# Hash attention and two MLPs on one core: the sums of weights leave GpSimd, and ScalarE scales the low words of float64

## The chip, the cores and the metric

The kernel runs on one NeuronCore of a Trainium2 chip. The metric is the device time of one execution in microseconds; for the kernel before it is the median of three runs. TensorE is PE in the profile, its weight loads are PEld, VectorE is DVE, ScalarE is ACT, GpSimd is POOL and the engine that issues the DMAs is SP. Every engine works through its own queue in order, so an instruction that waits holds everything behind it on that engine.

## The reference

Three parts follow each other. The first, an attention with a hash mask, gives `x` of 1536 tokens by 512. The second and the third are two MLPs, and the change lies in the second part, the first MLP, which also prepares the weights of the third.

```python
def _moe_ref(x, w_gate, w_val, w_out):            # first MLP: 512 -> 1536 -> 512
    g = x @ w_gate
    silu = g * (1.0 / (1.0 + np.exp(-g)))
    val = x @ w_val
    return (silu * val @ w_out).astype(np.float32)

def _moe2_ref(x, w_in, w_out, g_ln):              # second MLP: 512 -> 1024 -> 512
    h = x @ w_in
    e = np.exp(h - np.max(h, axis=-1, keepdims=True))
    solu = h * e / (np.sum(e, axis=-1, keepdims=True) + 1e-09)
    mu = np.mean(solu, axis=-1, keepdims=True)
    var = np.mean((solu - mu) ** 2, axis=-1, keepdims=True)
    ln = (solu - mu) / np.sqrt(var + 1e-06) * g_ln
    return (ln @ w_out).astype(np.float32)
```

The weights arrive as float64. The kernel computes each matmul as three matmuls of a high and a low part (high by high, high by low, low by high).

## The kernel before

**First MLP.** The hidden width of 1536 is cut into 12 columns of 128 (`f`), two to a stage, so there are six stages `t` = 0 to 5. The tokens are cut into three blocks of 512 (`blk`). A stage has nine units of 24 matmuls each: six hidden units (units 0 to 5: two `f` by three blocks, function `hidden`) and three sum units (`summed`, blocks 0 to 2), which multiply by `w_out`. PE runs the units one behind the other. A hidden unit fills two PSUM banks, `h0` (gate) and `h1` (value). ACT takes `silu` of `h0` (L1108), DVE multiplies by `h1` (L1109, written to `sg`), ACT rounds `sg` to `ah` (L1111), DVE forms the rest `al` (L1114). The bank pairs are doubled, so unit u+2 needs what unit u left to be read. A sum unit fills four banks `y`, one after the other, and there are only four, so the next sum unit needs them emptied: ACT copies them to `yf` in stage 0 (L1135), DVE adds them to `yf` in the later stages (L1137).

**Conversions.** Beside this runs a stream of weight conversions (`conversions`), cut into pieces of 1 MB of float64 each. Pieces "1" hold one `f` of `w_gate` and `w_val`, pieces "2" two `f` of `w_out`, pieces "3" 128 rows of the second MLP's `w_in`, pieces "4" 256 rows of its `w_out`. For each piece SP issues the load into `raw` (two buffers: the load of piece n+2 is issued when piece n is done), and `to_float32` makes float32 `wf` of it in six DVE instructions (L47, L51, L53, L57, L62, L64 by their profile names; L62 scales the low words, L64 adds them). Then ACT rounds to the high part (`hi`, L1037) and DVE forms the low part (`lo`, helper `low`, L958). The "late" pieces do more:

- Pieces "3" (`blocks3`, L960 to L993) also form sums and differences of weight blocks, `t1` to `t4`, each rounded to a high and a low part. GpSimd does the sums (L977 to L992) and the rounding (`rounded`, L1001 and L1002).
- Pieces "4" are scaled by `g_ln` (L1018), rounded by ACT (L1020), their low part is formed by GpSimd (L1021), and both parts are parked in DRAM (L1023), since they live in the piece's `raw` buffer.

**Order.** It is written out by hand: the main loop (the end of the listing's first MLP) takes steps of the stream with `go(stream)`, each step being what stands between two `yield`s of the conversion. A hidden unit takes up to four steps: one, then the `al` of the unit before, then up to three more that break off at a step that says "copied" (ACT's rounding), then silu, product and `ah` of the unit. A sum unit takes three steps, in stage 0 five. `LATE` says how many late pieces each stage gets, `late` in which order. Keys in `pieces` hold a piece back until its buffers are free: the first `f` of the next stage may start at unit 3, the second at the first sum unit.

**Ahead and behind.** At the end of the attention, PE, DVE and ACT each take one slot of about 2.1 us per block: ACT's exponential `e` (L574), PE's scores `s` (L539, two buffers), the transposes `t` (L589), ACT's `eh` (L598) and DVE's `el` (L602). Behind the first MLP, GpSimd forms sums of tokens (`sums_of`, L1001 to L1076) for the second MLP.

Of the kernel before, what the change touches and what calls it, by code (L numbers as in the profile page):

```python
# [9 lines left out]
F32 = mybir.dt.float32  # L10
R32 = mybir.dt.float32r
I32 = mybir.dt.int32
U32 = mybir.dt.uint32
# [21 lines left out]
FLOOR = 2.0 ** -15  # L35


def to_float32(nc, raw, f):

    words = raw.bitcast(I32).rearrange("p (n t) -> p n t", t=2)
    low, high = words[:, :, 0], words[:, :, 1]
    bits = f.bitcast(I32)


    nc.vector.tensor_scalar(  # L47
        bits, high, 1, 1, ALU.logical_shift_left, ALU.logical_shift_right
    )
    yield  # L50
    nc.vector.tensor_scalar_max(f, f, FLOOR)  # L51
    yield
    nc.vector.tensor_scalar(  # L53
        bits, bits, 3, 0x3FFFFFF8, ALU.logical_shift_left, ALU.bitwise_and
    )
    yield
    nc.vector.scalar_tensor_tensor(  # L57
        bits, high, -0x40000000, bits, ALU.bitwise_and, ALU.bitwise_or
    )
    yield  # L60

    nc.vector.tensor_scalar_mul(high, low.bitcast(U32), 2.0 ** -29)  # L62
    yield
    nc.vector.tensor_tensor(bits, bits, high, ALU.add)  # L64


@with_exitstack
def hash_attention_then_two_mlps(
# [150 lines left out]
    with at:  # L219
# [494 lines left out]
        def go(work):  # L714

            next(work, None)
# [182 lines left out]
    with ExitStack() as m1:  # L899
# [24 lines left out]
            nc.gpsimd.tensor_sub(lo[:, n], w1f[n], hi[:, n].bitcast(F32))  # L924

        pieces = []
        LATE = (2, 1, 1, 1, 1, 2)
        late = [("3", n) for n in (0, 2, 1, 3)] + [("4", n) for n in range(0, KF2, 2)]
        for t in range(TH):
            fs = range(t * FT, (t + 1) * FT)  # L930
            pieces += [(t - 1, FT * NBLK, "1", f) for f in fs[1:]]
# [25 lines left out]
        def low(dst, src, hi):  # L957
            nc.vector.tensor_sub(dst, src, hi.bitcast(F32))  # L958

        def blocks3(n, wf, raw):  # L960

            i, d = divmod(n, KH)
            left, right, other = wf[:, :BLK], wf[:, BLK:], w1f[d]
            b11, b21, b22, t1, t2, t3, t4 = (
                [w3_of[x][:, m, d] for m in range(2)]
                for x in ("b11", "b21", "b22", "t1", "t2", "t3", "t4")
            )
            add, sub = nc.gpsimd.tensor_add, nc.gpsimd.tensor_sub  # L970
            if i == 0:
                nc.scalar.copy(b11[0], left)
                nc.scalar.copy(other, right)
                yield "copied"
                low(b11[1], left, b11[0])
                one = raw.bitcast(F32)[:, :BLK]
                sub(one, other, b11[0].bitcast(F32))  # L977
                sub(one, one, b11[1].bitcast(F32))
                rounded(*t1, one)
                return  # L980
            nc.scalar.copy(b21[0], left)
            nc.scalar.copy(b22[0], right)
            yield "copied"
            low(b21[1], left, b21[0])
            sub(b22[1], right, b22[0].bitcast(F32))
            for block, first, t in ((b22, sub, t3), (b11, add, t2), (b21, sub, t4)):
                hi, lo = (x.bitcast(F32) for x in block)
                if first is sub:
                    sub(other, hi, other)
                else:  # L990
                    add(other, other, hi)
                add(other, other, lo)  # L992
                rounded(*t, other)  # L993

        def rounded(hi, lo, src):

# [7 lines left out]
        def convert(piece, raw):  # L1004
            kind, n = piece[2:4]
            wf = wr.tile([P, 2 * DM], F32, tag="wf", name="wf", bufs=1)
            yield from to_float32(nc, raw, wf)
            if kind == "4":

                hi, lo = (  # L1010
                    raw.bitcast(R32)[:, m * 2 * DM:(m + 1) * 2 * DM].rearrange(
                        "p (m e) -> p m e", m=2
                    ) for m in range(2)
                )
                wf = wf.rearrange("p (m e) -> p m e", m=2)
                both = lo.bitcast(F32)
                for m in range(2):
                    nc.scalar.mul(both[:, m], wf[:, m], gl[:, n + m:n + m + 1])  # L1018
                yield "copied"
                nc.scalar.copy(hi, both)  # L1020
                nc.gpsimd.tensor_sub(lo, both, hi.bitcast(F32))  # L1021
                for m, x in enumerate((hi, lo)):
                    nc.sync.dma_start(parked[m][n // 4][:, n % 4:n % 4 + 2], x.bitcast(F32))  # L1023
                return
            if kind == "3":
                yield from blocks3(n, wf, raw)
                return
            if kind == "1":
                hi, lo = weights1(n)
            else:  # L1030
                hi, lo = [
                    w2.tile([P, 2, DM], R32, tag=f"{x}2", name=f"{x}2") for x in ("hi", "lo")
                ]
                for m in range(2):
                    w2_of[n + m] = [x[:, m] for x in (hi, lo)]
            hi, lo = (x.rearrange("p m e -> p (m e)") for x in (hi, lo))
            nc.scalar.copy(hi, wf)  # L1037
            yield "copied"
            low(lo, wf, hi)
# [115 lines left out]
        for t in range(TH):  # L1155
            for unit in range((FT + 1) * NBLK):
                f, blk = divmod(unit, NBLK)
                reached = (t, unit)
                if t == TH - 1 and unit == FT * NBLK:

                    yh = xpool.tile([P, KD, NT], R32, tag="h", name="yh")
                    yl = xpool.tile([P, KD, NT], R32, tag="l", name="yl")
                    run(stream)
                    for n in (0, 2):
                        parts = halves(ws)
                        for x, stored in zip(parts, parked):
                            nc.sync.dma_start(x.bitcast(F32), stored[0][:, n:n + 2])
                        for m in range(2):
                            w4_of[n + m] = [x[:, m] for x in parts]
                    nc.scalar.activation(half, half, AF.Exp)  # L1170
                work = hidden(t * FT + f, blk) if f < FT else summed(t, blk)
                go(work)
                if f < FT:

                    go(stream)
                    go(before)
                    for _ in range(3):
                        if next(stream, None) == "copied":
                            break
                    go(work)  # L1180
                    before = work
                    continue

                go(before)
                before = lows(blk - 1) if t == TH - 1 and blk else iter(())
                for d in range(KD):
                    if blk and t == TH - 1:
                        go(before)
                    else:
                        if t == 0 or d != 1:  # L1190
                            go(stream)
                        if t == 0 and d == 1:
                            go(stream)
                    go(work)
# [265 lines left out]
```

## Time and profile before

| | |
|---|---|
| median of three runs | 700.08 us (698.76 to 700.26) |
| the profiled execution | 700.51 us, span of its instructions 698.7 us |
| attention | 0 to about 249 us |
| first MLP | about 248 to 559 us |
| second MLP | about 558 to 699 us |
| busy: PE, DVE, ACT, POOL | 679.0, 586.5, 354.8, 281.2 us |

Matmuls are pipelined: a matmul of 512 columns is shown with 0.39 us, but the next one starts 0.23 us later. So a busy PE says little; what counts is how far apart the starts of units lie, and which wait ended before a start that came late.

### The profile page before, as it was taken

What the parts mean: (1) busy time and instruction counts of PE and PEld (TensorE: products, weight loads), DVE (VectorE), ACT (ScalarE), POOL (GpSimd) and SP (SyncE); (2) the same over time, 40 slices, a digit from 0 to 9 for tenths busy, and PEclk for the clock granted to TensorE, in tenths of its full rate; (3) what the DMA queues carried; (4) which work ended last, traced back from release to release, by engine and by line L of the source; (5) the groups of instructions that cost most, each with busy time, mean ns of one, the idle gap of its engine ahead of it and who ended that gap; (6) DMA issues with size and microseconds to landing.
All of it is one profiled execution on the core that took longest, in us unless ns stands there. A gap on an engine that the chain in (4) does not pass through costs nothing. (4 is left out here: it accounts for less than half of the span.)

```text
span 698.7 us, 10396 instructions
## 1 busy us (share of the span) xinstructions
PE 679.0 (97%) x3653; PEld 583.0 (83%) x3653; DVE 586.5 (84%) x1032; ACT 354.8 (51%) x726; POOL 281.2 (40%) x285
## 2 busy tenths in 40 slices
PE   8999999999999999988899998999999999999998
PEld 6999999999998888866788886888888787888877
DVE  7989999999999997878897798886888869755781
ACT  7898898989888943332212202313222633433431
POOL 6647556666524340383030191000101575775300
PEclk9999999999999999999999999999999999999999
DMA  6683753736334112042131321243141530122211
GB/s 180 169 203 103 190 132 97 179 111 163 89 91 147 34 62 99 31 139 94 60 121 61 99 83 60 74 168 119 62 168 74 180 121 20 71 91 91 91 46 46
DMA packets 39492, 73.72 MB, mean 106 GB/s; under 512 B 5352, under 2 KB 26920, under 8 KB 38672
## 3 DMA queue, kind: packets, MB, share of 16 engines
q1 hardware_dynamic: 39440, 73.06, 34.1%
q8 instruction: 29, 0.48, 0.3%
q14 instruction: 23, 0.19, 0.1%
HBM read 40.90 MB, written 7.34 MB: 69 GB/s over the span
## 5 line engine op out<-in xcount | busy, mean ns | idle before, releaser
L1101 PE MATMUL h<-xh,hi 128*128 128x512 f32 x288 | 112.5, 391 | 6.4 <-ACT sg L1108 5.8
L1101 PE MATMUL h<-xl,hi 128*128 128x512 f32 x288 | 112.1, 389 | 0.0
L1101 PE MATMUL h<-xh,lo 128*128 128x512 f32 x288 | 111.2, 389 | 0.0
L602 DVE TENSOR_TENSOR el<-t,eh 128x384 fp32r<-128x384 f32 x192 | 97.7, 550 | 9.6 <-ACT eh L598 8.2
L574 ACT ACTIVATE e<-s,nm 128x768 f32<-128x768 f32 x96 | 97.7, 1017 | 4.5 <-DVE nm L559 3.8
L598 ACT CAST eh<-t 128x384 fp32r<-128x384 f32 x192 | 83.9, 492 | 18.5 <-PE t L589 16.8
L550 DVE TENSOR_REDUCE top<-s 128x1 f32<-128x768 f32 x96 | 90.6, 943 | 0.7 <-PE s L539 0.5
L589 PE MATMUL t<-idr,e 128*128 128x128 f32 x576 | 80.1, 274 | 0.5 <-DVE el L602 0.3
L589 PEld LDWEIGHTS t<-idr,e 128*128 128x128 f32 x576 | 67.9, 140 | 9.4 <-DVE el L602 4.0
L1101 PEld LDWEIGHTS h<-xh,hi 128*128 128x128 f32 x288 | 54.0, 188 | 19.2 <-ACT sg L1108 7.1
L624 PE MATMUL av<-eh,vs 128*128 128x384 f32 x186 | 63.9, 344 | 0.0
L1101 PEld LDWEIGHTS h<-xl,hi 128*128 128x128 f32 x288 | 54.1, 188 | 11.1
L1101 PEld LDWEIGHTS h<-xh,lo 128*128 128x128 f32 x288 | 54.0, 188 | 11.1
L1111 ACT CAST ah<-sg 128x512 fp32r<-128x512 f32 x36 | 22.4, 623 | 80.2 <-DVE sg L1109 80.2
L1037 ACT CAST hi<-wf 128x1024 fp32r<-128x1024 f32 x17 | 17.8, 1049 | 88.4 <-DVE wf L64 88.4
L1125 PE MATMUL y<-ah,hi 128*128 128x512 f32 x144 | 57.2, 397 | 4.9 <-DVE yf L1137 2.7
L1021 POOL TENSOR_TENSOR raw<-raw 128x1024 fp32r<-128x1024 f32 x4 | 9.8, 2441 | 118.4 <-ACT raw L1020 71.8
L1127 PE MATMUL y<-ah,lo 128*128 128x512 f32 x144 | 56.7, 394 | 0.0
L1126 PE MATMUL y<-al,hi 128*128 128x512 f32 x144 | 56.6, 393 | 0.0
L539 PE MATMUL s<-ka,qa 128*128 128x384 f32 x192 | 54.6, 365 | 1.6 <-ACT e L574 1.4
L628 PE MATMUL av<-el,vs 128*64 128x384 f32 x155 | 52.2, 337 | 0.0
L1109 DVE TENSOR_TENSOR sg<-h,sg 128x512 f32<-128x512 f32 x36 | 24.8, 688 | 30.7 <-ACT sg L1108 20.0
(277 smaller groups left out, 1585.6 us busy)
## 6 DMA issues: line engine op xcount, KB each, us to landing
raw<-in_moe_w_out_dram SPq DMA_DIRECT2D x10, 1024.0 KB
raw<-in_moe_w_gate_dram SPq DMA_DIRECT2D x12, 512.0 KB
raw<-in_moe_w_val_dram SPq DMA_DIRECT2D x12, 512.0 KB
ka<-kt SPq DMA_DIRECT2D x30, 192.0 KB
moved<-u SPq DMA_DIRECT2D x9, 512.0 KB
raw<-in_moe_w_in_dram SPq DMA_DIRECT2D x4, 1024.0 KB
parked<-raw SPq DMA_DIRECT2D x8, 512.0 KB
v<-in_v_dram SPq DMA_DIRECT2D x8, 384.0 KB
```

The costliest lines, as they stand in the source:

```text
L539: nc.tensor.matmul(s[:, n, :HALF], a[:, rows], m[:, n * HALF:(n + 1) * HALF], start=first, stop=not first,)
L550: nc.vector.tensor_reduce(top[:, 1:2], s_of[i][:, :, :HALF], AX.XY, ALU.max, negate=True)
L574: nc.scalar.activation(e, s_of.pop(i)[:, :, :HALF], AF.Exp, bias=nm[:, 1:2], scale=nm[:, 0:1], accum_out=total_of[p, n][:, j, c:c + 1],)
L589: nc.tensor.transpose(t[:, m, :], e_of[i][:, g, m * P:(m + 1) * P], idf)
L598: nc.scalar.copy(half_tile(eh_of, i, g), t_of[i, g])
L602: last_of[i] = nc.vector.tensor_sub(half_tile(el_of, i, g), t_of.pop((i, g)), half_tile(eh_of, i, g).bitcast(F32),)
L624: nc.tensor.matmul(av, vj[:, c], eh_of[h][:, c, :], start=c == 0, stop=c == C - 1)
L628: nc.tensor.matmul(*low, start=False, stop=False)
L1101: nc.tensor.matmul(ps[n], a[:, n, kk, :], x[:, kk, blk * BLK:(blk + 1) * BLK], start=kk == 0 and a is hi and x is xh, stop=kk == KD - 1 an ...
L1125: nc.tensor.matmul(p, hi[:, cols], ah, start=f == t * FT, stop=False)
L1126: nc.tensor.matmul(p, hi[:, cols], al, start=False, stop=False)
L1127: nc.tensor.matmul(p, lo[:, cols], ah, start=False, stop=f == (t + 1) * FT - 1)
```

## The change

- `to_float32` gets a switch. With it (all pieces of the first MLP), ACT scales the low words of `raw` in place as the first instruction of a piece, and DVE's L62 is gone. Without it (two small pieces in the attention) DVE still does it, now in place.
- `blocks3` forms all sums and differences on DVE, into `wf` and `w1f`, and ACT rounds them; GpSimd's instructions are gone. There are more `yield`s, so the work is cut into more steps.
- Pieces "4": ACT scales and rounds in one instruction for each half, DVE forms the low part with one instruction for each half.
- Late pieces come in another order: 30, 40 | 32 | 42, 44 | 31 | 33 | 46 by stage, where it was 30, 32 | 31 | 33 | 40 | 42 | 44, 46.
- A hidden unit now always takes four steps: those that a "copied" cut off come behind the unit's own work.

```diff
-def to_float32(nc, raw, f):
+def to_float32(nc, raw, f, scalar=False):
...
+    if scalar:
+        nc.scalar.mul(low, low.bitcast(U32), 2.0 ** -29)
     nc.vector.tensor_scalar(
         bits, high, 1, 1, ALU.logical_shift_left, ALU.logical_shift_right
     )
...
-    nc.vector.tensor_scalar_mul(high, low.bitcast(U32), 2.0 ** -29)
-    yield
-    nc.vector.tensor_tensor(bits, bits, high, ALU.add)
+    if not scalar:
+        nc.vector.tensor_scalar_mul(low, low.bitcast(U32), 2.0 ** -29)
+        yield
+    nc.vector.tensor_tensor(bits, bits, low, ALU.add)
...
-        LATE = (2, 1, 1, 1, 1, 2)
-        late = [("3", n) for n in (0, 2, 1, 3)] + [("4", n) for n in range(0, KF2, 2)]
+        LATE = (2, 1, 2, 1, 1, 1)
+        late = [(x[0], int(x[1])) for x in "30 40 32 42 44 31 33 46".split()]
...
-            add, sub = nc.gpsimd.tensor_add, nc.gpsimd.tensor_sub
+            add, sub = nc.vector.tensor_add, nc.vector.tensor_sub
             if i == 0:
                 nc.scalar.copy(b11[0], left)
                 nc.scalar.copy(other, right)
                 yield "copied"
                 low(b11[1], left, b11[0])
-                one = raw.bitcast(F32)[:, :BLK]
-                sub(one, other, b11[0].bitcast(F32))
-                sub(one, one, b11[1].bitcast(F32))
-                rounded(*t1, one)
+                yield
+                sub(left, right, left)
+                nc.scalar.copy(t1[0], left)
+                yield "copied"
+                low(t1[1], left, t1[0])
                 return
...
             low(b21[1], left, b21[0])
-            sub(b22[1], right, b22[0].bitcast(F32))
-            for block, first, t in ((b22, sub, t3), (b11, add, t2), (b21, sub, t4)):
...
+            yield
+            low(b22[1], right, b22[0])
+            yield
+            sub(right, right, other)
+            nc.scalar.copy(t3[0], right)
+            yield
+            add(other, right, b11[0].bitcast(F32))
+            yield
+            add(other, other, b11[1].bitcast(F32))
+            nc.scalar.copy(t2[0], other)
+            yield
+            low(t3[1], right, t3[0])
+            yield
+            sub(left, left, other)
+            nc.scalar.copy(t4[0], left)
+            yield
+            low(t2[1], other, t2[0])
+            yield "copied"
+            low(t4[1], left, t4[0])
...
-            yield from to_float32(nc, raw, wf)
+            yield from to_float32(nc, raw, wf, True)
...
-                    nc.scalar.mul(both[:, m], wf[:, m], gl[:, n + m:n + m + 1])
+                    nc.scalar.mul(hi[:, m], wf[:, m], gl[:, n + m:n + m + 1])
                 yield "copied"
-                nc.scalar.copy(hi, both)
-                nc.gpsimd.tensor_sub(lo, both, hi.bitcast(F32))
+                for m in range(2):
+                    if m:
+                        yield
+                    nc.vector.scalar_tensor_tensor(
+                        lo[:, m], wf[:, m], gl[:, n + m:n + m + 1], hi[:, m].bitcast(F32),
+                        ALU.mult, ALU.subtract,
+                    )
...
-                    for _ in range(3):
-                        if next(stream, None) == "copied":
-                            break
+                    steps = [go(stream)]
+                    while len(steps) < 3 and steps[-1] != "copied":
+                        steps.append(go(stream))
                     go(work)
+                    for _ in range(3 - len(steps)):
+                        go(stream)
```

PE's instructions stand in the same order as before. Three places show what moves on the others. Lines of the changed kernel are 2 or 3 higher than before up to `blocks3`, and 14 to 20 higher behind it.

The first place is ACT near the end of the attention, ten exponentials before the last. Before, its queue there reads:

```order
L691 COPY xf<-av 128x384
L598 CAST eh<-t 128x3x128 x2
L574 ACTIVATE e,total<-s,nm 128x768
L598 CAST eh<-t 128x3x128 x2
L574 ACTIVATE e,total<-s,nm 128x768
```

and now:

```order
L694 COPY xf<-av 128x384
L601 CAST eh<-t 128x3x128 x2
L48 ACTIVATE raw<-raw 128x1024
L577 ACTIVATE e,total<-s,nm 128x768
L601 CAST eh<-t 128x3x128 x2
```

The first piece's scaling (L48) has come between `eh` and an exponential; the DVE half of that piece still starts only when the attention's last `el` is done.

The second place is ACT in the sum units of stage 0, where ACT itself empties the banks `y`. Before, from unit 5's silu on (piece 30 gives `w3b` and `w1f`, piece 32 the next two `w3b`):

```order
L1108 ACTIVATE sg<-h_4200 128x512
L1111 CAST ah<-sg 128x512
L1135 COPY yf<-y 128x512
L972 CAST w3b_3963<-wf 128x512
L973 COPY w1f_96<-wf 128x512
L1135 COPY yf<-y 128x512 x6
L981 CAST w3b_3964<-wf 128x512
L982 CAST w3b_3965<-wf 128x512
L1135 COPY yf<-y 128x512 x5
```

and now (`w3t` is a sum of weights, `raw<-wf,gl` the scaling of piece 40, `hi` the rounding of a piece "1"):

```order
L1126 ACTIVATE sg<-h_4207 128x512
L1129 CAST ah<-sg 128x512
L981 CAST w3t_3966<-wf 128x512
L1153 COPY yf<-y 128x512
L48 ACTIVATE raw<-raw 128x1024
L1153 COPY yf<-y 128x512 x4
L1031 ACTIVATE raw<-wf,gl 128x512 x2
L1153 COPY yf<-y 128x512 x2
L48 ACTIVATE raw<-raw 128x1024
L1153 COPY yf<-y 128x512 x3
L1055 CAST hi_4370<-wf 128x1024
L1153 COPY yf<-y 128x512 x2
```

The first copy now stands behind the rounding of a sum, and scalings and roundings of three more pieces lie between the other copies.

The third place is GpSimd, whose queue before had this between the attention's last `xl` and the sums of tokens, a second time for the other half, and four `raw<-raw` behind it (the start is shown); all of it is gone:

```order
L977 TENSOR_TENSOR raw<-w1f,w3b 128x512
L978 TENSOR_TENSOR raw<-raw,w3b 128x512
L1001 TENSOR_TENSOR w3t<-raw,unit 128x512
L1002 TENSOR_TENSOR w3t<-raw,w3t 128x512
L985 TENSOR_TENSOR w3b<-wf,w3b 128x512
L989 TENSOR_TENSOR w1f<-w3b,w1f 128x512
L992 TENSOR_TENSOR w1f<-w1f,w3b 128x512
```

On DVE the sums of pieces 32 and 33 now lie between the additions to `yf` of a stage's sum units, which in stage 1 reads:

```order
L961 TENSOR_TENSOR w3b_3965<-wf,w3b_3965 128x512
L1155 TENSOR_TENSOR yf<-y,yf 128x512 x2
L992 TENSOR_TENSOR wf<-wf,w1f_96 128x512
L1155 TENSOR_TENSOR yf<-y,yf 128x512
L995 TENSOR_TENSOR w1f_96<-wf,w3b_3963 128x512
L1155 TENSOR_TENSOR yf<-y,yf 128x512
L997 TENSOR_TENSOR w1f_96<-w1f_96,w3b_3963 128x512
```

Each step between two additions is one instruction of 128x512 there, where steps of 128x1024 stood.

## Rows read from the trace of the kernel before

**Rows 1.** The page: busy us, share of the span and instructions, by engine.

```profile
PE 679.0 (97%) x3653; PEld 583.0 (83%) x3653; DVE 586.5 (84%) x1032; ACT 354.8 (51%) x726; POOL 281.2 (40%) x285
```

**Rows 2.** Timeline of PE, unit starts: start us, us shown, engine, line, operation, names.

```profile
255.00 0.39 PE L1101 MATMUL h<-xh,hi 128*128 128x512 f32 x1
...
369.62 0.39 PE L1101 MATMUL h<-xh,hi 128*128 128x512 f32 x1
...
375.06 0.39 PE L1101 MATMUL h<-xh,hi 128*128 128x512 f32 x1
...
553.12 0.39 PE L1125 MATMUL y<-ah,hi 128*128 128x512 f32 x1
```

**Rows 3.** Waits of PE, 248 to 560 us: us in total, times, longest.

```profile
PE h L1101 <- ACT sg L1108: 5.8, 3, 2.6
PE y L1125 <- DVE yf L1137: 2.7, 2, 1.9
PE y L1125 <- ACT yf L1135: 2.2, 2, 2.0
PE h L1101 <- DVE sg L1109: 0.6, 1, 0.6
```

**Rows 4.** Windows: length, busy us (instructions) PE, PEld, DVE, ACT, POOL; clock; DMA.

```profile
301.00:359.00 58.00, 52.35 (x221) 41.82 (x220) 51.65 (x56) 11.82 (x19) 25.35 (x16) 0.97 0.21 70
359.00:408.00 49.00, 49.00 (x218) 40.58 (x217) 39.58 (x51) 11.22 (x17) 8.04 (x6) 1.00 0.29 101
```

**Rows 5.** The same view, one stretch behind a wait of PE.

```profile
345.00:350.00 5.00, 3.88 (x12) 3.08 (x13) 4.92 (x8) 0.97 (x2) 0.00 (x0) 0.74 0.00 0
```

**Rows 6.** Timeline of POOL in stage 1.

```profile
305.14 1.62 POOL L1002 TENSOR_TENSOR w3t<-w1f,w3t 128x512 fp32r<-128x512 f32 x1
```

**Rows 7.** Timeline of DVE beside it.

```profile
305.65 2.20 DVE L57 SCALAR_TENSOR_TENSOR wf<-raw,wf 128x1024 int32<-128x1024 int32 x1
```

**Rows 8.** Timeline of DVE, such instructions in stage 0, POOL idle.

```profile
260.20 0.69 DVE L51 TENSOR_SCALAR wf<-wf 128x1024 f32<-128x1024 f32 x1
260.81 0.68 DVE L1109 TENSOR_TENSOR sg<-h,sg 128x512 f32<-128x512 f32 x1
...
262.80 1.22 DVE L57 SCALAR_TENSOR_TENSOR wf<-raw,wf 128x1024 int32<-128x1024 int32 x1
264.05 0.69 DVE L62 TENSOR_SCALAR raw<-raw 128x1024 int32<-128x1024 uint32 x1
264.78 1.23 DVE L64 CUSTOM_DVE_ANT_0 wf<-raw,wf 128x2048 uint16<-128x2048 uint16 x1
...
267.62 0.69 DVE L1109 TENSOR_TENSOR sg<-h,sg 128x512 f32<-128x512 f32 x1 [1.61 <-ACT sg L1108]
```

**Rows 9.** Timeline of ACT, sum units of stage 0; in brackets idle time and its end.

```profile
298.16 0.62 ACT L981 CAST w3b<-wf 128x512 fp32r<-128x512 f32 x1 [5.13 <-DVE wf L64]
```

**Rows 10.** Groups of ACT by form, 255 to 558 us: busy, mean ns, idle before.

```profile
L1037 ACT CAST hi<-wf 128x1024 fp32r<-128x1024 f32 x17 | 17.8, 1049 | 88.4 <-DVE wf L64 88.4
L1018 ACT ACTIVATE raw<-wf,gl 128x512 f32<-128x512 f32 x8 | 5.4, 716 | 16.9 <-DVE wf L64 16.9
```

**Rows 11.** Groups of DVE by form, 255 to 558 us.

```profile
L958 DVE TENSOR_TENSOR w3b<-wf,w3b 128x512 fp32r<-128x512 f32 x4 | 2.8, 693 | 1.5 <-ACT w3b L972 0.7 <-ACT w3b L981 0.7
```

**Rows 12.** Timeline of ACT where the first scaling will stand.

```profile
222.82 0.87 ACT L598 CAST eh<-t 128x384 fp32r<-128x384 f32 x2
223.56 1.03 ACT L574 ACTIVATE e<-s,nm 128x768 f32<-128x768 f32 x1
```

**Rows 13.** Timeline of PE there, the scores that reuse that exponential's buffer.

```profile
225.06 0.59 PE L539 MATMUL s<-ka,qa 128*128 128x384 f32 x2
```

**Rows 14.** Timeline of SP: the load of the first piece is issued.

```profile
219.04 0.54 SPq L944 DMA_DIRECT2D raw<-in_moe_w_gate_dram  x1
```

**Rows 15.** Windows of 1 us there; the last figure is GB/s moved.

```profile
223.00:224.00 1.00, 1.00 (x9) 0.93 (x8) 0.97 (x4) 1.00 (x3) 0.00 (x0) 1.00 1.04 319
```

**Rows 16.** Waits of PE in the second MLP.

```profile
PE o L1330 <- DVE ll L1316: 0.7, 2, 0.5
```

More of the change, by code (lines that the diff above doesn't have):

```diff
@@ L958, in low, with blocks3 @@
             nc.vector.tensor_sub(dst, src, hi.bitcast(F32))
-        def blocks3(n, wf, raw):
+        def blocks3(n, wf):
             i, d = divmod(n, KH)
@@ L984, in blocks3 @@
             low(b21[1], left, b21[0])
-            sub(b22[1], right, b22[0].bitcast(F32))
-            for block, first, t in ((b22, sub, t3), (b11, add, t2), (b21, sub, t4)):
[L987 to L993, printed above, removed]
+            yield
[17 more added lines that the diff above has]
+            low(t4[1], left, t4[0])
         def rounded(hi, lo, src):
@@ L1015, in convert @@
                 wf = wf.rearrange("p (m e) -> p m e", m=2)
-                both = lo.bitcast(F32)
                 for m in range(2):
-                    nc.scalar.mul(both[:, m], wf[:, m], gl[:, n + m:n + m + 1])
+                    nc.scalar.mul(hi[:, m], wf[:, m], gl[:, n + m:n + m + 1])
                 yield "copied"
-                nc.scalar.copy(hi, both)
-                nc.gpsimd.tensor_sub(lo, both, hi.bitcast(F32))
+                for m in range(2):
[5 more added lines that the diff above has]
+                    )
                 for m, x in enumerate((hi, lo)):
@@ L1025, in convert @@
             if kind == "3":
-                yield from blocks3(n, wf, raw)
+                yield from blocks3(n, wf)
                 return
```

## The prediction

> **What bounds the kernel now.** I began with the page [rows 1]. PE is busy for 97% of the span, but that counts the pipelined tail of each matmul, so I went on to unit starts [rows 2]. An undisturbed hidden unit takes 375.06 - 369.62 = 5.44 us for its 24 matmuls. From the second unit of the first MLP (255.00) to its last sum unit (553.12) lie 52 units. At 5.44 us they would take 282.9 us; they took 298.1. So the first MLP loses 15.2 us, and nothing that leaves PE's 24 matmuls as they are can give back more there.
>
> The list of waits [rows 3] says who is late: 5.8 + 2.7 + 2.2 + 0.6 = 11.3 us of PE's waits end with ACT's silu or copy or with DVE's product or addition. The other 3.9 us follow the waits: a matmul behind one takes longer to get going, and behind the wait at 346 us the granted clock falls to 0.74 for a stretch [rows 5], that is, part of it at 1.2 GHz.
>
> Why they are late shows in the windows. In stage 1, with POOL busy for 25 us, DVE is busy for 51.7 of 58 us and PE waits; in stage 2, with POOL busy for 8 us, DVE is busy for 39.6 of 49 and PE doesn't wait [rows 4]. A single instruction shows it: L57 takes 1.22 us alone [rows 8] and 2.20 us beside POOL [rows 7]. It began at 305.65, POOL's L1002 ended at 306.76 [rows 6], and 2.20 - 1.22 = 1.0 us of it lies before that. The two alternate, and DVE runs at about half speed for as long as POOL has sums to form. ACT stands in order behind it: its rounding waited 5.13 us for DVE [rows 9], with the copies that PE needed queued behind.
>
> **The change, part by part.**
>
> GpSimd's sums go. All of POOL's work of the first MLP's weights (34 instructions of 128x512 and four of 128x1024, counted in its queue) disappears, and with it the doubling of DVE's instructions.
>
> DVE's own load. Each of 24 pieces loses one L62 of 0.69 us [rows 8], 16.6 us in all. Added are sums and low parts of 128x512: 2 for a piece 30 or 31, 8 for 32 or 33, 2 for each of four pieces "4", so 2x2 + 2x8 + 4x2 = 28 at 0.69 [rows 11], 19.3 us. The two balance. An ordinary piece now costs DVE about 5.9 us: L47, L51, L53 at 0.73 from start to start, L57, L64 and `lo` at 1.25 [rows 8]. Stage 1 has three of these, piece 32 (4.7 + 9 x 0.69 = 10.9 us), and at 0.69 each six products with their rests and twelve additions (16.6): 45.2 us of the 48.96 that nine units last. Stage 2, with two pieces "4" (6.1 each) in place of it, has 46.5. Both fit.
>
> ACT's load. Each piece gains a scaling of 128x1024. No row has ScalarE on integer words with a stride. From below, the rounding of 128x1024 takes 1.05 us; from above I take twice the two scalings of 128x512 at 0.72 each with a second pass, 2.3 us [rows 10]. I take 1.15, since the scaling of 512 costs 0.1 more than its share of the rounding. ACT is busy for 11.8 of 58 us in stage 1 [rows 4], so as load it costs nothing; what counts is what stands behind it. The Trainium skill ("ScalarE: Activation LUTs", section "Rules for kernel authors") speaks against this move: multiplications belong on VectorE. By the same page's section "What ACT_TABLE_LOAD costs" an instruction with immediate operands would take an estimated 186 + 0.833 x 1024 = 1040 ns, so the sum below would be 0.1 us lower; that it is longer than DVE's 0.69 agrees with the rows, and it matters only where ACT is the one awaited.
>
> That is the **attention's end**, the first new cost. The scaling of the first piece comes to ACT at 223.56, when the exponential started [rows 12]. Its load was issued at 219.04 [rows 14]; by the bytes moved in windows of 1 us, of which the last that counts is [rows 15], its 1 MB is there at about 223.9. So the scaling runs from 223.95 to 225.1, the exponential ends at 226.1, and the scores that need its buffer start then and not at 225.06 [rows 13]: 1.05 us. `eh` behind it gives 0.15 more. PE has no gaps in that part, so this is lost: **+1.2 us** (0.9 with a scaling of 1.05 and no more, 2.6 with 2.3 us and the load 0.3 later).
>
> **Stage 0's sum units** keep part of their stall. The first copy of a bank now stands on ACT behind the rounding of piece 30's difference. From the end of that piece's L64 the chain is, at 0.62 for an ACT instruction of 128x512 [rows 9] and 0.6 to 0.7 for one of DVE (0.61 where the next doesn't depend on it, 260.20 to 260.81 in [rows 8]): two roundings, silu, product, low part, rest, difference, rounding, copy, some 5.6 us; the next sum unit wants the bank 5.3 us after unit 5 ends. So the stall is how late that L64 ends, plus 0.3. DVE starts this stage late: at its beginning ACT now rounds piece "1" and loads its table ahead of the first silu. A unit asks DVE for four of a piece's six steps (3.9 us) and 1.2 of product and rest, 5.1 of 5.44, and where a rounding stands ahead of a silu it idles another 1.6 [rows 8]. I walked the three queues by hand in their new order with these durations: L64 ends 1.4 us after unit 5. That gives 1.7 us, and 0.2 for a second bank: **1.9 us left** (0.3 with no delay, 4.4 with 4).
>
> **Stages 1 to 4.** The same chain ends in an addition on DVE without the extra rounding; the pieces held back to unit 3 let DVE catch up first. The walk gives the first bank 0.3 us before it is wanted, 0.1 in stage 2. I leave **0.6 us** for the four (0 to 3). The other copies and silus have 3 to 4 us to spare. The load of the piece behind a "4" waits until both halves are parked; the walk has it land 3 us before a silu behind its scaling is due.
>
> **Second MLP.** GpSimd's sums of tokens start as soon as the last low parts of block 0 are there, now about 0.8 us earlier against PE. PE's 0.7 us behind `ll` [rows 16] may shrink: **-0.4** (0 to -0.7).
>
> **Sum.** Against the profiled execution of 700.51 us: -15.2 + 1.9 + 0.6 + 1.2 - 0.4 = -11.9, so 688.6. The median lies 0.43 lower, 700.08: **688.2 us**.
>
> **The rivals.**
>
> *Scaling on ScalarE is dear* (2.3 us). For it: strided integer words, which no row has; against it: DVE reads the same words at its usual 0.69 [rows 8]. The attention loses 1.15 more, and in stage 0 the second copy comes 1.2 later than its bank is wanted. 688.2 + 2.3 = 690.5, up to 694 with other copies late.
>
> *The queues, not the doubling, make PE wait.* For it: 8 of the 11.3 us end with ACT [rows 3], and three more conversions now lie between the copies of stage 0. Against it: stage 2 has the same queues and no wait [rows 4]. Half of the 15.2 us stays, 7.6 where the forecast leaves 2.5: 688.2 + 5.1 = 693.3.
>
> *Slower: ACT turns into the bound.* Every scaling stands ahead of a silu. In the 1.5 units of a piece, 8.16 us, ACT has one rounding (1.05, [rows 10]) and 1.5 times silu and `ah` (at 0.62 each 1.9), so 5.2 us are free. Should an integer scaling take more, PE waits for the excess 24 times: at 7 us, 24 x 1.8 = 43, about 731. It decides the sign from 5.7 us on (24 x 0.5 = 12). Against it: a rounding of the same size takes 1.05 us. A load that lands later than 8 us after its issue would act the same way.
>
> *It doesn't do what it says:* what the sums give, waits on loads behind parked pieces take back; about 700.
>
> **How the numbers follow.** Forecast 0.62, dear scaling 0.15, queues 0.10, slower 0.08, no change 0.05. What a measurement can tell apart is 0.2%, 1.4 us. The first three are faster: 0.87; same 0.05; slower 0.08. The forecast's own bounds: against 700.08, -15.2 + 0.3 + 0.9 - 0.7 = -14.7, so 685.4; and -15.2 + 4.4 + 3 + 2.6 = -5.2, so 694.9. That takes in the first two rivals but for their tails. The range is 685 to 695.5.
>
> **What would show it.** Right: DVE's L57 and its like at 1.22 us through stages 1 and 3; PE's waits in the first MLP about 2 us, nearly all in stage 0 at a `y` bank; clock 1.00 throughout; scores about 1 us late once at 225 us; the scaling at 1.1 to 1.2 us. Wrong: a scaling over 2 us; PE waiting in stages 1 to 4 for a silu behind a scaling; or DVE's instructions still stretched with POOL idle.

## The result and the profile after

The changed kernel takes 689.54 us (median of four, 687.92 to 690.89), the kernel before 699.42 in the same comparison: ratio 0.986 [0.983, 0.989]. Timed again it was 688.68 against 701.36, 0.982 [0.980, 0.984]. Its profiled execution took 687.92 us, 12.6 less than the 700.51 of before. Below, the page of the changed kernel: its busy line (to compare with [rows 1]), POOL's slices of the span, and the chain that ended last. A line of the changed kernel has a number 2 to 20 higher than the same line before.

```profile
PE 675.5 (98%) x3653; PEld 582.4 (85%) x3653; DVE 563.5 (82%) x1035; ACT 381.8 (56%) x755; POOL 216.7 (32%) x247
...
POOL 6647555666624260000000000000000574775200
...
PE 85%; DVE 8%; ACT 3%; issue 2%; DMA 1%; POOL 0%; SPq 0%; ACTq 0%; DVEq 0%; POOLq 0%
```

POOL is idle through the first MLP, and the chain is PE's own work for 85%. The waits of PE in the first MLP are down from four groups with 11.3 us [rows 3] to one:

```profile
PE y L1143 <- ACT yf L1153: 1.8, 1, 1.8
```

The windows of stages 1 and 2 (length; busy PE, PEld, DVE, ACT, POOL; clock; DMA) have PE busy throughout at clock 1.00, where stage 1 had 58 us [rows 4]:

```profile
299.00:348.00 49.00, 49.00 (x218) 40.58 (x217) 38.21 (x51) 19.56 (x29) 0.00 (x0) 1.00 0.34 117
348.00:397.00 49.00, 49.00 (x218) 40.58 (x217) 41.86 (x55) 16.67 (x23) 0.00 (x0) 1.00 0.31 108
```

**One number for each kernel.** As in the prediction, the loss of the first MLP is the time from the start of its second unit to that of its last sum unit, less 52 x 5.44 = 282.9 us. Before it was 15.2. Now the two starts are 255.83 and 540.97, and the loss is 2.26. The table gives it by stage for every run below. Time and ratio come from all runs of a kernel, the loss from its one traced execution. By time alone neither the kernel with fills nor the one with the sums back on GpSimd can be told from the changed kernel, since their intervals overlap; the loss tells them apart. From "changed, again" on, each four ran on one chip with their own runs of the kernel before (medians 701.36, 700.38 and 700.44 us); the ratios are against these.

| kernel | time, us | ratio [95%] | loss by stage 0 to 5 | sum |
|---|---|---|---|---|
| before | 699.42 | 1 | 2.8, 8.5, 0, 2.9, 0, 1.1 | 15.2 |
| changed | 689.54 | 0.986 [0.983, 0.989] | 2.3, 0, 0, 0, 0, 0 | 2.3 |
| changed, again | 688.68 | 0.982 [0.980, 0.984] | 2.3, 0, 0, 0, 0, 0 | 2.3 |
| first scaling on DVE | 690.92 | 0.985 [0.983, 0.986] | 5.0, 0, 0, 0, 0, 0 | 5.0 |
| rounding later | 685.90 | 0.979 [0.977, 0.980] | 0.1, 0, 0, 0, 0, 0 | 0.1 |
| both of these | 686.58 | 0.979 [0.977, 0.981] | 1.4, 0, 0, 0, 0, 0 | 1.4 |
| idle GpSimd additions | 705.44 | 1.007 [1.003, 1.011] | 7.4, 2.2, 1.5, 6.4, 2.1, 0.5 | 20.1 |
| idle GpSimd fills | 690.24 | 0.985 [0.981, 0.989] | 4.5, 0, 0, 0, 0, 0 | 4.5 |
| sums back on GpSimd | 690.41 | 0.985 [0.981, 0.989] | 4.3, 0, 0.2, 0, 0, 0 | 4.5 |
| before + scaling on ACT | 697.54 | 0.995 [0.994, 0.997] | 6.6, 1.4, 3.1, 0, 0, 0 | 11.0 |
| before + new order | 697.28 | 0.995 [0.993, 0.997] | 5.5, 2.1, 0.2, 1.6, 1.8, 0.3 | 11.4 |
| changed, old list | 693.53 | 0.990 [0.988, 0.992] | 2.3, 5.0, 0, 0, 0, 0 | 7.3 |
| changed, no scaling on ACT | 692.90 | 0.989 [0.988, 0.991] | 1.1, 0, 0, 3.9, 0, 3.4 | 8.4 |
| five scalings | 745.76 | 1.064 [1.062, 1.066] | 18.5, 7.6, 9.9, 9.3, 7.7, 4.1 | 57.1 |

### The profile page after: what moved, and what is told of

It reads as the page before. It is cut to its first block, busy times and chain, and to the rows that moved or that the text cites. A ratio compares the mean times of both kernels' runs of the same rounds, so it can differ in the third digit from the quotient of the medians.

```text
span 686.1 us, 10380 instructions
## 1 busy us (share of the span) xinstructions
PE 675.5 (98%) x3653; PEld 582.4 (85%) x3653; DVE 563.5 (82%) x1035; ACT 381.8 (56%) x755; POOL 216.7 (32%) x247
## 4 chain that ended last, share of the span: by engine, by line
PE 85%; DVE 8%; ACT 3%; issue 2%; DMA 1%; POOL 0%; SPq 0%; ACTq 0%; DVEq 0%; POOLq 0%
PE h L1119 24%; PE s L542 9%; PE t L592 8%; PE h L1235 7%; PE y L1143 5%; PE y L1144 4%; PE y L1145 4%; PE av L627 4%; PE av L631 3%; PE o L1350 3%; PE o L1348 3%; PE o L1349 3%; PE pp L501 2%; PE pp L458 2%; PE t L1329 1%
## 5 line engine op out<-in xcount | busy, mean ns | idle before, releaser
L605 DVE TENSOR_TENSOR el<-t,eh 128x384 fp32r<-128x384 f32 x192 | 97.8, 551 | 10.7 <-ACT eh L601 9.4
L1082 POOL TENSOR_TENSOR sf<-yh 128x256 f32<-128x256 f32 x5 | 3.7, 736 | 282.2 <-ACT yh L1158 282.2
L542 PE MATMUL s<-kb,qb 76*128 76x384 f32 x192 | 49.8, 339 | 0.0
```

Of the source, the lines that this page charges most:

```text
L542: nc.tensor.matmul(s[:, n, :HALF], a[:, rows], m[:, n * HALF:(n + 1) * HALF], start=first, stop=not first,)
L605: last_of[i] = nc.vector.tensor_sub(half_tile(el_of, i, g), t_of.pop((i, g)), half_tile(eh_of, i, g).bitcast(F32),)
```

## Experiments on what is left: the attention's end and stage 0

> The changed kernel as it is, timed again beside the three below, so that differences of a microsecond can be read on one chip. By its first times 687.9 to 690.9 us, ratio 0.983 to 0.989. PE's waits in the first MLP: once 1.75 us at 290.39 in front of a sum unit of stage 0, nothing in stages 1 to 5. Any other picture would say that the first trace was no typical one.

The picture is the same: one wait of 1.8 us, loss 2.25.

**The rounding in stage 0.** The timeline of ACT in the changed kernel shows the chain that the one wait ends with (start, us, engine, line, operation, names; in brackets idle time and what ended it), and behind it the matmul that waited:

```profile
284.86 0.62 ACT L975 CAST w3b<-wf 128x512 fp32r<-128x512 f32 x1 [3.15 <-DVE wf L67]
285.39 0.61 ACT L976 COPY w1f<-wf 128x512 f32<-128x512 f32 x1
285.91 0.59 ACT L1126 ACTIVATE sg<-h 128x512 f32<-128x512 f32 x1
287.26 0.62 ACT L1129 CAST ah<-sg 128x512 fp32r<-128x512 f32 x1 [0.76 <-DVE sg L1127]
289.24 0.62 ACT L981 CAST w3t<-wf 128x512 fp32r<-128x512 f32 x1 [1.36 <-DVE wf L980]
289.76 0.58 ACT L1153 COPY yf<-y 128x512 f32<-128x512 f32 x1
```

```profile
290.39 0.50 PE L1143 MATMUL y<-ah,hi 128*128 128x512 f32 x1 [1.75 <-ACT yf L1153]
```

The rounding L981 waits 1.36 us for DVE's difference L980, and the copy that PE needs stands behind it. The next kernel moves difference and rounding three steps back.

```diff
                 yield
+                for _ in range(3 if n == 0 else 0):
+                    yield
                 sub(left, right, left)
                 nc.scalar.copy(t1[0], left)
```

> The changed kernel, but the difference of the first block of weights (piece 30) and its rounding on ScalarE are formed three steps later, so that the copies of stage 0's first banks no longer stand behind the rounding. My theory: the 1.75 us wait of PE at 290.4 goes (0.3 or less left), and 1.8 to 2.2 us less than the changed kernel, about 0.3%. Rival (queues as such): something else of the same queue is late next, the next bank or silu, and half of it or more comes back: 0 to 1 us less. Second rival: the delayed piece pushes the next pieces into units of stage 1 and PE waits there: no gain or a loss.

```profile
287.27 0.62 ACT L1131 CAST ah<-sg 128x512 fp32r<-128x512 f32 x1 [0.76 <-DVE sg L1129]
287.80 1.07 ACT L1155 COPY yf<-y 128x512 f32<-128x512 f32 x2
289.25 0.62 ACT L983 CAST w3t<-wf 128x512 fp32r<-128x512 f32 x1 [0.39 <-DVE wf L982]
```

In the same view, two copies now stand ahead of the rounding, the list of PE's waits in the first MLP is empty, and the loss is 0.09. The median is 2.8 us below that of the changed kernel on the same chip, the profiled span 2.3. Nothing came back later. This is the lowest median measured, 685.90 us.

**The first scaling.** The next kernel leaves the first piece's scaling on DVE.

```diff
-            yield from to_float32(nc, raw, wf, True)
+            yield from to_float32(nc, raw, wf, None if piece == pieces[0] else True)
```

(`to_float32` takes no extra step for it.)

> The changed kernel, but the low words of the very first piece are scaled by VectorE, in the step of the instruction before it. My theory: ScalarE's scaling at 223.82 us holds the exponential behind it back by 1.3 us and so the scores by 0.9 us; without it the exponential starts at about 223.6, the scores at 225.06 and the first MLP 0.8 us earlier: 0.9 us less than the changed kernel (0.13%). Rival: the load that lands late at this place is what counts, or the 0.9 us were lost anyway in what follows; then the time is the changed kernel's within 0.2 us, or longer because VectorE's own queue in the attention is late by 0.7.

> Both edits of the two kernels above together. If they are independent, as I think, the gains add: 2.7 to 3.1 us less than the changed kernel, about 686 to 687 us, with no wait of PE above 0.7 us from 246 us to the second MLP. If VectorE, now with one more instruction in the attention, comes later into stage 0, the stall of stage 0 stays and only 0.9 us is gained.

The attention does get its time back: with both edits the first MLP starts at 248.16, with the rounding moved alone at 249.09, 0.93 earlier. But the kernel with this edit alone isn't faster. DVE has L65 as one instruction more at the first MLP's door:

```profile
254.23 1.50 DVE L65 TENSOR_SCALAR raw<-raw 128x1024 int32<-128x1024 uint32 x1
```

Against PE's end of the unit, DVE's products in stage 0 then come 1.3 us later than in the changed kernel, and PE's one wait grows from 1.8 to 3.1 us:

```profile
PE y L1144 <- ACT yf L1154: 3.1, 1, 3.1
```

Behind that wait the clock falls, which it didn't behind the 1.75 (windows of the kernel with the scaling on DVE):

```profile
290.00:294.00 4.00, 2.12 (x6) 1.68 (x7) 3.21 (x6) 3.27 (x6) 0.00 (x0) 0.79 0.22 76
294.00:300.00 6.00, 6.00 (x25) 4.83 (x24) 4.97 (x7) 4.01 (x7) 0.00 (x0) 0.86 0.15 63
```

So 0.9 us are gained and 2.7 lost (loss 4.99 against 2.26). The rival named in the expectation, DVE's own queue, was right. With the rounding moved as well, 0.9 are gained and 1.3 lost. That kernel is 2.1 us below the changed one, where I had expected 2.7 to 3.1.

## Experiments on the cause: GpSimd, DVE's load or the order

**GpSimd beside DVE.** Two kernels let GpSimd work on blocks of weights that nobody waits for, once with additions, once with fills.

```diff
                 low(b11[1], left, b11[0])
+                for _ in range(4):
+                    nc.gpsimd.tensor_add(w1f[1 - d], w1f[1 - d], b11[0].bitcast(F32))
...
             low(b21[1], left, b21[0])
+            for _ in range(13):
+                nc.gpsimd.tensor_add(w1f[1 - d], w1f[1 - d], b21[0].bitcast(F32))
```

> The changed kernel, and beside it GpSimd adds blocks of weights (128x512, float32) into a tile that nobody reads before it is written anew: four additions after piece 30 and 31 each, thirteen after 32 and 33 each. Nothing of the other engines' work or order is changed. My theory (VectorE's instructions are stretched for as long as GpSimd reads operands beside them): VectorE's conversions take about 2.2 us instead of 1.2 beside it, VectorE is late and PE's waits in stages 1 and 3 come back: 5 to 10 us more than the changed kernel, 694 to 700 us. Rival (the queues, not the doubling, made PE wait): nothing waits for GpSimd here, so the time is the changed kernel's, within 1 us, with VectorE's instructions as before the additions.

> The same as the kernel with GpSimd's idle additions, but GpSimd fills the tile with zeros instead: it writes and reads nothing. It tells which of GpSimd's accesses VectorE shares. If reading is what counts: VectorE's two-operand instructions stay at 0.69 and 1.23 us and the time is the changed kernel's within 1 us. If any GpSimd access counts: VectorE stretched as with the additions, 694 to 700 us. A fill may also be shorter than an addition, so I read the duration of the VectorE instructions that lie within it, not the total alone.

The additions bring the loss to 20.1 us, more than it was before the change; that is 17.8 above the changed kernel, where I had expected 5 to 10. Beside four of them on POOL (first row), DVE's two-operand instructions with both operands in SBUF take 1.63 to 1.76 us in place of 0.69. The product `sg`, which reads one operand from a PSUM bank, is as fast as ever, 0.69:

```profile
442.67 6.01 POOL L980 TENSOR_TENSOR w1f<-w1f,w3b 128x512 f32<-128x512 f32 x4 [81.66 <-ACT w3b L975]
```

```profile
443.64 0.69 DVE L1131 TENSOR_TENSOR sg<-h,sg 128x512 f32<-128x512 f32 x1 [1.70 <-ACT sg L1130]
444.25 1.63 DVE L961 TENSOR_TENSOR w3b<-wf,w3b 128x512 fp32r<-128x512 f32 x1
445.81 1.76 DVE L1136 TENSOR_TENSOR al<-sg,ah 128x512 fp32r<-128x512 f32 x1
447.49 1.74 DVE L982 TENSOR_TENSOR wf<-wf 128x512 f32<-128x512 f32 x1
```

The additions to `yf` read a bank too, and in stage 1, beside thirteen additions of POOL, two of them take 1.27:

```profile
339.35 21.67 POOL L992 TENSOR_TENSOR w1f<-w1f,w3b 128x512 f32<-128x512 f32 x13 [48.04 <-ACT w3b L987]
```

```profile
345.86 1.27 DVE L1159 TENSOR_TENSOR yf<-y,yf 128x512 f32<-128x512 f32 x2
```

The place counts for more than the number. Four additions in stages 0 and 3 raise the loss there by 5.2 and 6.4 us, thirteen in stages 1 and 4 by 2.2 and 2.1.

PE's longest waits are back on DVE's additions and ACT's copies:

```profile
PE y L1147 <- DVE yf L1159: 8.4, 4, 3.5
PE y L1147 <- ACT yf L1157: 4.7, 1, 4.7
```

The fills waited for nothing and ran early, thirteen of them in one block from 258.09 to 266.92. There DVE's instructions with two operands keep their 0.69 and 1.22, and those with one operand, L49 to L55, take 0.98 to 1.10 in place of 0.69:

```profile
258.09 8.83 POOL L992 MEMSET w1f<- 128x512 f32 x13
```

```profile
261.12 1.22 DVE L961 TENSOR_TENSOR lo<-wf,hi 128x1024 fp32r<-128x1024 f32 x1
262.72 0.69 DVE L1136 TENSOR_TENSOR al<-sg,ah 128x512 fp32r<-128x512 f32 x1
263.32 1.10 DVE L49 TENSOR_SCALAR wf<-raw 128x1024 int32<-128x1024 int32 x1
264.46 0.98 DVE L53 TENSOR_SCALAR wf<-wf 128x1024 f32<-128x1024 f32 x1
```

That is 1.0 us of DVE's time; PE's wait in stage 0 grew by as much, to 2.7 us, and with the lower clock behind it the loss to 4.5. The time is 1.6 us above the changed kernel's, a little more than the 1 us expected. So what stretches a two-operand instruction is GpSimd's reading. The Trainium skill ("SBUF — State Buffer", section "Who interferes with whom") says the same: an instruction with two SBUF operands contends with a GpSimd instruction that reads, not with one that only writes; one with at most one SBUF operand doesn't, outside modes that a one-operand `tensor_scalar` can enter. The rows agree: 1.63 to 1.76 beside the additions, 0.69 and 1.22 beside the fills, 0.69 with a bank as operand.

**The sums back on GpSimd.** By the prediction, this part of the change was the gain. The next kernel undoes it alone.

```diff
-            add, sub = nc.vector.tensor_add, nc.vector.tensor_sub
+            add, sub = nc.gpsimd.tensor_add, nc.gpsimd.tensor_sub
...
-                sub(left, right, left)
-                nc.scalar.copy(t1[0], left)
...
+                sub(one, other, b11[0].bitcast(F32))
+                sub(one, one, b11[1].bitcast(F32))
+                rounded(*t1, one)
...
```

> The changed kernel, but the sums of weights of the four pieces 3 go back to GpSimd as in the kernel before; the scaling on ScalarE, the new order of pieces and the products of pieces 4 stay as changed. My theory (the doubling is the cause): though VectorE has 20 instructions of 0.69 us less to do (13.8 us), it is stretched while GpSimd sums, and PE's waits in stages 1 and 3 return: 693 to 697 us. Rival (order and VectorE's own load are the cause): VectorE has less to do than in the changed kernel, so the time is the changed kernel's or 1 us less.

My theory missed: 690.4 us, and no loss in stages 1, 3, 4 and 5. POOL is busy with sums again, in stage 1 for 14.9 us. But they fall beside the sum units, where DVE has only additions to `yf` left, and those aren't stretched (POOL, then DVE):

```profile
339.60 1.75 POOL L995 TENSOR_TENSOR w1f<-w3b,w1f 128x512 f32<-128x512 f32 x1
341.43 1.63 POOL L998 TENSOR_TENSOR w1f<-w1f,w3b 128x512 f32<-128x512 f32 x1
```

```profile
340.17 1.73 DVE L1127 TENSOR_TENSOR al<-sg,ah 128x512 fp32r<-128x512 f32 x1
341.82 2.47 DVE L1150 TENSOR_TENSOR yf<-y,yf 128x512 f32<-128x512 f32 x4
```

One instruction of those is stretched (`al`, 1.73), at a place where DVE has time to spare. The loss in stage 0, 2.1 us more than in the changed kernel, stands at another bank: ACT's copy there is behind the scaling of piece 40, which waited 4.79 us for DVE. DVE is late there beside GpSimd's sums of piece 30: L49, L53 and L55 of piece 40's conversion, with one operand each, take 1.80, 1.41 and 1.66 us in place of 0.69, 2.8 us more in all (POOL, DVE, ACT):

```profile
291.23 1.37 POOL L1010 TENSOR_TENSOR w3t<-raw,unit 128x512 fp32r<-128x512 f32 x1
```

```profile
289.90 1.80 DVE L49 TENSOR_SCALAR wf<-raw 128x1024 int32<-128x1024 int32 x1
291.74 1.41 DVE L53 TENSOR_SCALAR wf<-wf 128x1024 f32<-128x1024 f32 x1
293.18 1.66 DVE L55 TENSOR_SCALAR wf<-wf 128x1024 int32<-128x1024 int32 x1
```

```profile
297.50 1.34 ACT L1026 ACTIVATE raw<-wf,gl 128x512 fp32r<-128x512 f32 x2 [4.79 <-DVE wf L67]
```

PE waits 2.3 us for that copy, and the clock falls behind it (0.91 and 0.75 in two windows of 5 us). In stage 0, then, the stretching does cost time. That is read from this trace; no run takes the stretching away there and leaves the rest.

**One part alone, and one part missing.** After this I replaced the theory by a budget: DVE's work in a stage, stretched where GpSimd reads, against the 48.96 us of nine units. Two kernels add one part to the kernel before, two take one from the changed kernel.

Before, with the scaling on ACT alone (`to_float32(nc, raw, wf, True)` and nothing else):

> The kernel before with one part of the change alone: ScalarE scales the low words, so that each piece needs six steps of VectorE and not seven. GpSimd's sums, the order of pieces and the steps per unit stay as before. My theory: VectorE loses 25 x 0.69 = 17 us of load over the first MLP, which lets it catch up sooner behind each stretch with GpSimd, but the stretch stays: half of the gain, 693 to 697 us. Rival (VectorE's load was the cause, not the doubling): nearly the whole gain, 689 to 691 us. Third: no gain, or a loss, since pieces done earlier meet the same stretch: 699 to 702.

Before, with the new list of late pieces and the four steps of a unit alone:

> The kernel before with the order alone changed: the list of late pieces, how many each stage gets, and that a unit always takes three steps of VectorE. GpSimd's sums and VectorE's scaling stay. After the run with the sums back on GpSimd (690.4 us) I no longer hold that the stretched VectorE instructions cost time by themselves; the theory is now a budget: VectorE's own work, stretched, against the 48.96 us that nine units of a stage last, and the order decides in which stage the stretch falls. By it, this kernel has the four pieces 3 in stages 0, 1, 3 and 4, one each, and loses where one meets three ordinary pieces of 6.6 us: 3 us in stage 0, 3 in stage 1, 2 to 3 in stage 4, in all 8 to 10 of the 15.2: 693 to 696 us. Rival (the order is the whole gain): 690 to 691. Second rival (the order is worth nothing while GpSimd sums): 699 to 701.

The changed kernel with the old list:

```diff
-        LATE = (2, 1, 2, 1, 1, 1)
-        late = [(x[0], int(x[1])) for x in "30 40 32 42 44 31 33 46".split()]
+        LATE = (2, 1, 1, 1, 1, 2)
+        late = [("3", n) for n in (0, 2, 1, 3)] + [("4", n) for n in range(0, KF2, 2)]
```

> The changed kernel with the old list of late pieces (30 and 32 in stage 0, then 31, 33, 40, 42, 44 and 46) and the rest as changed. Budget theory: stage 0 gets 4.8 us more of VectorE's work than with the new list (9 instead of 2 extra instructions of 0.69 us), and it ends late already; PE's loss in stage 0 rises from 2.3 us to 5 to 7, stage 1 has less and loses little: 692 to 695 us. Rival (where the pieces stand doesn't matter once GpSimd has none): 688.7 us as changed, within 1 us.

The changed kernel with the scaling on DVE:

```diff
-            yield from to_float32(nc, raw, wf, True)
+            yield from to_float32(nc, raw, wf)
```

> The changed kernel without the scaling on ScalarE: VectorE scales the low words itself, so each piece has seven steps instead of six and VectorE 25 x 0.69 = 17 us more to do. Budget theory: stage 0, which is late already, gets 5 x 0.69 = 3.5 us more and loses 5 to 6 us instead of 2.3; stage 1 needs 48.0 and stage 2 50.0 of 48.96, so 1 us is lost there; the attention gets its 0.9 us back: 691.5 to 694.5 us. Rival (only VectorE's stretch beside GpSimd cost time in the kernel before): nothing is lost and the attention's 0.9 us comes back: 688 us.

Scaling alone or order alone takes 4 of the 15.2 us each. Both times lie above what was expected, by 0.5 us (scaling) and 1.3 us (order). About half of what the new order leaves, 5.5 of 11.4 us, stands in stage 0, where 3 were expected. As in the kernel with the sums back on GpSimd, piece 40's conversion lies there beside the sums of piece 30, its scaling waits for DVE, and a copy that PE waits 3.5 us for stands behind (DVE, then ACT, of the kernel before with the new order):

```profile
295.45 2.20 DVE L57 SCALAR_TENSOR_TENSOR wf<-raw,wf 128x1024 int32<-128x1024 int32 x1
```

```profile
299.67 1.33 ACT L1018 ACTIVATE raw<-wf,gl 128x512 f32<-128x512 f32 x2 [6.50 <-DVE wf L64]
```

With the scaling alone, where 6.6 of 11.0 us stand in stage 0, it is piece 32's rounding that waits, 5.75 us. In stages 1 and 4 of the new order alone DVE, which still scales, comes late to the sum units and has conversions left beside GpSimd's sums. They are stretched there, and the additions that PE waits for stand behind them (DVE):

```profile
346.07 1.76 DVE L47 TENSOR_SCALAR wf<-raw 128x1024 int32<-128x1024 int32 x1 [0.59 <-POOL w3b L985]
347.75 0.68 DVE L1137 TENSOR_TENSOR yf<-y,yf 128x512 f32<-128x512 f32 x1
```

Scaling and order together, the kernel with the sums back on GpSimd, take 10.7 (15.2 less 4.5). It also has the new form of the pieces "4", which no run separates. From the other end, without the scaling the loss rises by 6.1, without the new list by 5.0, without the sums on DVE by 2.3. Without the scaling PE waits in another place than I wrote, for the low parts of the next stage's weights, which DVE finishes too late. With the old list the wait that is added is for an addition of stage 1; in stage 0 it stays 1.8 us (PE's waits, one row of each):

```profile
PE h L1119 <- DVE lo L961: 3.2, 2, 1.6
```

```profile
PE y L1143 <- DVE yf L1155: 3.3, 1, 3.3
```

Both times fell into the ranges expected by the budget, but the stages didn't, so it gives the size and not the place. The sums on DVE alone, in the old order and with DVE scaling, weren't run.

**A long scaling.** The last kernel has five scalings in place of one; the four added multiply by 1.0.

> The changed kernel with five scalings on ScalarE for each piece instead of one (four more that multiply the same words by 1.0, in place, same operands): 5.8 us ahead of each conversion. It puts a price on the rival in which ScalarE becomes the bound. By the sum that rival was made from, ScalarE then needs 1.05 + 1.9 + 5.8 = 8.7 us for each 8.16 us of 1.5 units: 0.5 to 0.6 us lost on each of 24 pieces, 13 us, and 4.6 us more at the attention's end: about 706 us. If a long scaling holds up silus and copies behind it before ScalarE is full, more: stage 0's copies alone come 4.6 us later for each bank they stand behind a scaling for, 710 to 720. If the scalings run in time that ScalarE has to spare and nothing waits for it: 693 us, the attention's 4.6 us alone.

It took 745.8 us, 40 more than the sum for that rival. ACT is far from full, 38 of 49 us in a window across the end of stage 0 and the start of stage 1, so it isn't the bound (window, then waits of DVE and of PE):

```profile
299.00:348.00 49.00, 41.44 (x167) 33.26 (x168) 29.15 (x36) 38.12 (x47) 0.00 (x0) 0.91 0.28 99
```

```profile
DVE sg L1129 <- ACT sg L1128: 68.3, 29, 3.5
...
DVE wf L69 <- ACT raw L50: 7.6, 3, 4.0
```

```profile
PE y L1145 <- DVE yf L1157: 24.1, 4, 7.6
PE y L1145 <- ACT yf L1155: 12.7, 3, 8.0
PE h L1121 <- ACT sg L1128: 3.8, 2, 2.2
```

DVE waits for silus and scalings behind these blocks of 5.8 us, DVE's additions queue up behind, and PE waits 40.6 us for banks. The other 16.5 of the 57.1 us go with a granted clock of 0.91 to 0.93 from 299 to 546 us. The attention's end cost 3.2 (first MLP from 252.27).

## Why the prediction was right, and where its reason was not

The time was right, 688.2 against 689.54, and the terms of the sum came out near, though not all for the reason given:

- *Attention*, +1.2 predicted: the first MLP starts 0.83 later. The scaling came 0.1 earlier than I wrote, took 1.16 us, and the exponential behind it could begin 0.1 before its end:

```profile
223.82 1.16 ACT L48 ACTIVATE raw<-raw 128x1024 int32<-128x1024 uint32 x1
224.87 0.97 ACT L577 ACTIVATE e<-s,nm 128x768 f32<-128x768 f32 x1
```

```profile
225.99 0.62 PE L542 MATMUL s<-ka,qa 128*128 128x384 f32 x2 [0.70 <-ACT e L577]
```

- *The scaling's price*, 1.15 between 1.05 and 2.3: 25 of them (the prediction counted 24), 1154 ns on average. The rival of the dear scaling falls.

```profile
L48 ACT ACTIVATE raw<-raw 128x1024 int32<-128x1024 uint32 x25 | 28.8, 1154 | 1.8 <-DMA raw<-in_moe_w_out_dram 1.6
```

- *Stage 0*, 1.9 left: 2.26, at the bank and behind the rounding that the walk of the queues named; the moved rounding showed it.
- *Stages 1 to 4*, 0.6 left: 0.
- *Second MLP*, -0.4: from 553.12 and 540.97 to the ends of the spans it is 145.6 and 145.1, so -0.45. The reason given isn't shown: the kernels before with one part alone, where GpSimd still forms sums of weights, have 145.1 and 145.2 as well.
- *From profile to median*: taken as -0.43 as before, it was +1.6. The profiled execution was the fastest of its four, at 687.92 where the sum gave 688.6: the attention and stages 1 to 4 were put 0.4 and 0.6 too high, stage 0 0.4 too low. So two misses of opposite sign, 0.7 and 2.0, leave the 1.3 us between 688.2 and 689.54; that much is luck.

The step that failed is the reason of the largest term. "GpSimd's sums go ... and with it the doubling of DVE's instructions" was given the whole 15.2 us. The doubling is real: additions that nobody waits for cost 17.8 us when DVE is as loaded as in the changed kernel. But with the scaling on ACT and the new order, the sums on GpSimd cost 2.3, in a kernel whose DVE is also spared 13.8 us of work; 10.7 of the 15.2 us go without moving them. PE waited where DVE's queue was late, by its own work and by the stretching together: in stage 0 a conversion beside the sums, as the prediction read it from the wait of 5.13 us [rows 9], in other stages also plain work at the wrong moment. Three parts each take something from it: ACT takes 17 us of work, the new list moves the sums to where DVE reads PSUM or has time left, and the sums on DVE end the stretching. How much the last would give by itself stays open, since it wasn't run alone. The prediction counted the first as a mere balance for DVE's added sums (16.6 against 19.3) and gave the order no term. The total came out right because all parts were made together and a loss can't fall below zero.

The rival *queues, not the doubling* was right about the place of what remained, though not about its size (2.3 us and not 7.6): 1.75 us of plain order on ACT, which three steps of delay removed. The *slower* rival was priced wrongly. Free time on ACT, 5.2 us for each piece, is not the margin of a queue in order, and at 5.8 us the excess wasn't 0.6 us on each piece but 57.1 in all. Where between 1.15 and 5.8 us it begins wasn't tried.

## What to carry to other kernels

When several parts are changed at once and the sum of their effect is bounded (a stall that can only go to zero), a right total says little about the parts: undo each alone before naming the cause. A co-processor that slows another engine costs time only where that engine's queue is late, so look at which instructions lie beside it (here, instructions that read PSUM weren't slowed) before moving its work. A copy that frees a bank for PE belongs ahead of any instruction in its queue that waits for a third engine.

## What the hardware showed that I had not expected

- Beside GpSimd's reading additions, a DVE instruction of 128x512 with one operand in a PSUM bank keeps its 0.69 us while one with both operands in SBUF takes up to 1.76. Beside GpSimd's sums in stage 0, one-operand instructions of 128x1024 take 1.41 to 1.80 in place of 0.69. Beside GpSimd's fills, only DVE's one-operand instructions are slower, 0.98 to 1.10 in place of 0.69.
- The price of a wait of PE isn't its length. The wait of 1.75 us cost 2.3 at clock 1.00; the one of 3.1 us cost 5.0, with 0.79 and 0.86 behind it, that is, part of the time at 1.2 GHz.
- In five of the fourteen traces, of five different kernels, the clock granted in the first 20 us is 0.91 and not 1.00. In the three of them that are variants of the changed kernel, the first MLP starts 1.1 to 1.4 us later than with the same attention at 1.00 (at 250.51 and not 249.09 in the kernel with fills), so I compared stretches within the first MLP. The row is from the windows of that kernel:

```profile
0.00:20.00 20.00, 17.01 (x92) 13.87 (x93) 16.07 (x52) 13.51 (x27) 12.37 (x25) 0.91 0.56 160
```
